# Own PSUM banks for the shift row, Wo's first product copied into the second's banks, and a new hand-kept order of all engines

## The chip, the cores and the metric

The kernel runs on one core of a Trainium2 chip. The metric is the device time of one execution in microseconds, median over runs. All times below are microseconds (us) unless marked otherwise. Engines are named as in the profile: PE (TensorE, matmuls), DVE (VectorE), ACT (ScalarE), POOL (GpSimd, which here mostly issues DMAs and does small steps), SP (SyncE, which issues DMAs).

## What is computed

One transformer block with adaptive LayerNorm: S = 2048 rows, D = 1024 columns, 32 heads, F = 3584.

```python
mod = silu(c) @ w_mod                      # six vectors: sa, ca, ga, sb, cb, gb
h = layernorm(x) * (1 + ca) + sa
q, k, v = split_heads(h @ wqkv)            # 32 heads of 32
pq, pk = phi(q), phi(k)                    # phi(t) = (t + 1 if t > 0 else exp(t)) + 1e-6
kv = sum over s of pk[s] (x) v[s];  z = sum over s of pk[s]
o = (pq @ kv) / (pq @ z + 1e-6)
x = x + ga * (o @ wo)
h = layernorm(x) * (1 + cb) + sb
x = x + gb * ((gelu(h @ w_gate) * (h @ w_up)) @ w_down)
```

Inputs and outputs are bfloat16.

## The kernel before

**Phases.** The code runs `kvq_phase` (first LayerNorm, K, V, K/V products per head, Q), `merge_phase` (numerators and denominators of the attention), `wo_phase` (output projection, residual, second LayerNorm), and then for each of two groups of 1024 rows `gate_up(g)` and `down_out(g)`. The 2048 rows are four blocks b = 0 to 3 of 512 rows; a group is two blocks. Most large products are not done as eight half-size block products but as seven (`seven`, with stages `s1` to `s7`), with sums and differences of blocks made beforehand by DVE. In the feed-forward part some of the seven are split in seven once more. So PE has fewer matmuls, and DVE has many additions (line 788, the helper `tt_op`, which records every addition of two tensors).

**PSUM.** It has eight banks of 512 fp32 columns. `Banks(lo, hi)` is a ring over some of them: each call hands out the next. Two rings that share a bank make their users wait for each other. `psK0 = Banks(4, 7)` is the ring of the K products of block 0 (`k_group`: eight matmuls at line 1248, then ACT takes Exp at 1254 and Relu at 1255, and DVE adds them). `psR` is the ring of `shift_row`; before, it is bank 7 alone.

**Shift row.** V of the first block is multiplied without the additive part `sa` of the modulation. `shift_row` makes up for it: DVE spreads `sa` (line 1034), sixteen matmuls (`row_sums`, line 860) multiply it with Wv, ACT copies the row, and two adds (`add(0)`, `add(1)`: one matmul at line 1042 and four DVE steps each) put it on the K/V sums. All three take their bank from `psR`.

**Modulated columns.** `hr1[0]` is the first block's normalized input, transposed; at the end of `start_phase` its eight column tiles are scaled and shifted, by DVE (line 1028) or for every third tile by ACT. The K groups of block 0 read them. Beside them, `ln1_block(1)` makes statistics of the next block (lines 866 and 868).

**Wo.** Blocks 0 and 1 go through `wo_tile`, eight plain tiles (matmuls at line 1526), each followed by ACT and DVE statistics and a normalized copy. Those copies go to DRAM scratch `xhs` and come back transposed (`h2_load`, line 1462, one load for each half of the group), and are then modulated in `h2_mod` (ACT at line 1504, DVE at 1506) into the operand of gate and up. Blocks 2 and 3 go through `wo_stages`, a seven-product (matmuls at line 1590). `QA`, `QB`, `QC`, `QD` are the bank pairs 0-1, 2-3, 4-5, 6-7. In `s1` the first product P1 is made in pair A, and ACT copies it (`fcopy`, line 1093, 1024 fp32 columns) to SBUF; A is then kept and accumulated on. In `s2` the second product is made in pair B, and `comb` adds P1 from SBUF to it (DVE, PSUM and SBUF) and that sum to the residual (DVE, SBUF only). In `s3` A is accumulated on and copied once more (`fcopy`). `s5` copies each half at line 1125.

**Gate, up, down.** `gate_up` uses lines 1705 (plain products) and 1716 (the products split once more), with seeds from one PSUM bank to another by ACT (line 1761) and Gelu at 1780; `down_out` uses lines 1921 and 1966 and ends with the output.

**Order.** The code doesn't issue as it runs. `Plan` records each instruction with what it reads and writes; `Plan.order` plans all five engines with a cost for each kind of instruction, and `Plan.refine` then moves instructions by hand-kept tables, `SHIFTS`: for each engine a list that says for each place by how many places the instruction that stands there was moved ("z13" stands for thirteen zeros). The instructions are issued in that order on each engine, with semaphore waits where one depends on another. So on each engine the order is fixed, and an instruction that waits holds back all behind it on its engine. Two instructions on the same engine also wait for each other by semaphore where the second reads what the first wrote.

Of the kernel before, what the change touches and what calls it, by code (L numbers as in the profile page):

```python
# [508 lines left out]
def kernel(  # L509
# [581 lines left out]
    def fcopy(ring, ps):  # L1091
        t = ring()
        ac.activation(out=t, in_=ps, func=AF.Copy)  # L1093
        return t

    def seven(mm, comb, direct, A, B, slots=(0, 1, 2), ring=None):


        st = {}
# [8 lines left out]
        def s1():  # L1108
            st["pa"] = products(A.pair(), "a11", "b11", True)
            st["p1"] = fcopy(p1_at, st["pa"])  # L1110
# [1082 lines left out]
```

## Time and profile before

| | us |
|---|---|
| runs | 737.71, 737.94, 739.62 |
| median | 737.94 |
| the profiled execution | 738.96 |
| its span on the core | 737.2 |
| mean granted PE clock in it | 0.997 |

The profiled execution is the one that all rows are from; its span is from the first instruction to the last, the rest of its time lies around that. The timeline's rows give start and duration in us from the span's start, the engine, the line, the operation, output and input, shapes and count, and in brackets the idle time before it and what ended it. Neighbouring rows of the same kind are drawn together (x36). A matmul row's end is modelled, so the next row can start before it. "L788" is the line of the helper for additions, whoever calls it.

### The profile page before, as it was taken

How to read it: one execution, taken by the hardware profiler on the slowest of the kernel's cores; microseconds unless marked ns; L12 is line 12 of the kernel's file. 1: busy time of each engine (PE TensorE's matmuls, PEld its weight loads, DVE VectorE, ACT ScalarE, POOL GpSimd, SP SyncE). 2: the span in 40 equal slices, each digit the busy share in tenths (PEclk: the TensorE clock that was granted, in tenths of full speed). 3: DMA queues.
4: the chain of work that ended last, by engine and by line, in shares of the span. 5: the costliest groups of instructions: out<-in, count | busy, mean ns of one | idle time of the engine just before them, and what ended most of it. 6: DMA issues, size and time to landing. Idle time of an engine off the chain costs nothing.

```text
span 737.2 us, 12148 instructions
## 1 busy us (share of the span) xinstructions
PE 724.6 (98%) x4365; PEld 404.5 (55%) x4365; DVE 658.0 (89%) x1472; ACT 457.3 (62%) x829; POOL 103.2 (14%) x174
## 2 busy tenths in 40 slices
PE   8999999999999999999999999999999999999997
PEld 4444545444444555555555667545555555568674
DVE  5699998797799999999997799987897899999998
ACT  5566666679787799999776712026677776742110
POOL 2325631120121012311300000000000010000000
PEclk9999999999999999999999999999999999999999
DMA  9976855999999477768867788645242455599992
GB/s 313 329 200 161 240 102 126 312 275 280 303 249 315 174 226 239 190 203 255 240 176 246 208 278 270 219 168 175 91 140 103 140 175 175 169 258 284 269 278 86
DMA packets 160988, 159.26 MB, mean 216 GB/s; under 512 B 34208, under 2 KB 140448, under 8 KB 160288
## 3 DMA queue, kind: packets, MB, share of 16 engines
q1 hardware_dynamic: 143568, 122.30, 55.4%
q0 software_dynamic: 14848, 33.82, 15.3%
q10 hardware_dynamic: 2512, 2.36, 1.0%
q8 instruction: 34, 0.56, 0.3%
q14 instruction: 26, 0.21, 0.1%
HBM read 122.42 MB, written 36.04 MB: 215 GB/s over the span
## 4 chain that ended last, share of the span: by engine, by line
PE 78%; DVE 13%; issue 3%; DMA 2%; ACT 2%; POOL 1%; DVEq 0%; SPq 0%; ACTq 0%; POOLq 0%
PE psum L1705 28%; PE psum L1716 10%; PE psum L1921 8%; DVE mem L788 8%; PE psum L1966 8%; PE psum L1149 8%; PE psum L1219 7%; PE psum L1526 3%; PE psum L1590 2%; PE psum L923 2%; DVE mem L866 1%; DMA mem<-xhs 1%; PE psum L1263 1%; DMA xhs<-mem 1%; PE psum L1248 1%
## 5 line engine op out<-in xcount | busy, mean ns | idle before, releaser
L788 DVE TENSOR_TENSOR mem<-mem 128x256 f16<-128x256 f16 (+14 forms) x857 | 380.8, 486 | 19.9 <-ACT mem L1093 4.5
L1705 PE MATMUL psum<-mem 128*128 128x512 f16 x1144 | 273.9, 379 | 0.0
L1093 ACT ACTIVATE mem<-psum 128x512 f32<-128x512 f32 (+3 forms) x320 | 167.4, 557 | 131.6 <-PE psum L1966 36.8
L788 DVE TENSOR_TENSOR mem<-psum,mem 128x512 f16<-128x512 f32 (+5 forms) x213 | 159.8, 757 | 23.5 <-PE psum L1149 7.3
L1705 PEld LDWEIGHTS <-mem 128*128 128x128 f16 (+1 forms) x1144 | 111.7, 98 | 102.8 <-issue 1.4
L1716 PE MATMUL psum<-mem 128*128 128x256 f16 x742 | 106.9, 272 | 0.9 <-DVE mem L788 0.6
L1716 PEld LDWEIGHTS <-mem 128*128 128x128 f16 (+1 forms) x742 | 72.3, 98 | 43.9 <-issue 2.6
L1966 PE MATMUL psum<-mem 128*128 128x256 f16 (+1 forms) x784 | 88.7, 273 | 0.2 <-ACT mem L1093 0.2
L1966 PEld LDWEIGHTS <-mem 128*128 128x128 f16 x784 | 76.6, 98 | 12.8 <-DVE mem L788 0.4
L1921 PE MATMUL psum<-mem 128*128 128x512 f16 (+2 forms) x350 | 75.2, 370 | 1.0 <-DVE mem L788 1.0
L1149 PE MATMUL psum<-mem 128*128 128x512 f16 (+1 forms) x280 | 63.2, 379 | 0.0
L788 DVE TENSOR_TENSOR psum<-psum,mem 128x256 f32<-128x256 f32 x106 | 44.8, 429 | 15.9 <-ACT mem L1093 9.5
L1761 ACT ACTIVATE psum<-psum 128x512 f32<-128x512 f32 x56 | 32.6, 584 | 38.3 <-DVE mem L788 26.5
L1921 PEld LDWEIGHTS <-mem 128*128 128x128 f16 x350 | 34.2, 98 | 37.0 <-issue 1.2
L1219 PE MATMUL psum<-mem 128*128 128x512 f16 x224 | 51.6, 379 | 0.0
L1149 PEld LDWEIGHTS <-mem 128*128 128x128 f16 x280 | 27.1, 98 | 32.1 <-DVE mem L1052 0.4
L1780 ACT ACTIVATE mem<-psum 128x512 f16<-128x512 f32 x56 | 33.1, 597 | 10.3 <-PE psum L1705 10.0
L1219 PEld LDWEIGHTS <-mem 128*128 128x128 f16 (+1 forms) x224 | 21.5, 98 | 25.7 <-issue 0.8
L1790 ACT ACTIVATE mem<-mem 128x512 f16<-128x512 f16 x56 | 34.9, 631 | 0.8 <-DVE mem L788 0.8
L1327 POOL DMA_DIRECT2D ts<-in_B_w_down_dram x28 | 29.0, 1335 | 6.9 <-DMA ts<-in_B_w_down_dram 6.5
L1248 PE MATMUL psum<-mem 128*128 128x512 bf16 x128 | 29.6, 379 | 0.2
L1526 PE MATMUL psum<-mem 128*128 128x512 f16 x128 | 28.2, 379 | 0.0
(143 smaller groups left out, 577.4 us busy)
## 6 DMA issues: line engine op xcount, KB each, us to landing
mem<-in_B_w_gate_dram SPq DMA_DIRECT2D x14, 1024.0 KB, 7.8
mem<-in_B_w_up_dram SPq DMA_DIRECT2D x14, 1024.0 KB, 6.0
mem<-in_w_mod_dram SPq DMA_DIRECT2D x24, 512.0 KB, 8.5
mem<-us SPq DMA_DIRECT2D x24, 448.0 KB, 8.7
mem<-ts SPq DMA_DIRECT2D x5, 1792.0 KB, 9.4
ts<-in_B_w_down_dram POOLq DMA_DIRECT2D x28, 256.0 KB, 6.5
mem<-in_B_w_down_dram SPq DMA_DIRECT2D x15, 448.0 KB, 6.4
mem<-in_A_x_dram SPq DMA_DIRECT2D x23, 256.0 KB, 5.7
```

Source lines behind the costliest of these rows:

```text
L788: ve.tensor_tensor(out=out, in0=a, in1=b, op=op)
L1093: ac.activation(out=t, in_=ps, func=AF.Copy)
L1149: te.matmul(ps, lhsT=A[:, k, i * P:(i + 1) * P], rhs=B[:, k, :], start=(start and k == 0), stop=(k == KH - 1), skip_group_check=True)
L1219: te.matmul(o, lhsT=W[:, k, (j0 + i) * P:(j0 + i + 1) * P], rhs=h_form(a, k), start=(start and k == 0), stop=(k == KH - 1), skip_group_che ...
L1248: te.matmul(ps, lhsT=hr1[b][:, k, tl * P:(tl + 1) * P], rhs=Wk[:, k, n * NW:(n + 1) * NW], start=(k == 0), stop=(k == KD - 1))
L1526: te.matmul(psw[:, half, :], lhsT=pqT[b][:, g, tl * P:(tl + 1) * P], rhs=Wp[:, g, half * NW:(half + 1) * NW], start=(g == 0), stop=(g == K ...
L1705: te.matmul(ps, lhsT=a[:, k, e, :], rhs=b[:, k, :], start=(start and k == 0), stop=(k == KH - 1), skip_group_check=True)
L1716: te.matmul(ps, lhsT=self.x[a][:, k, :], rhs=self.y[y][:, k, :], start=(start and k == 0), stop=(k == KH // 2 - 1), skip_group_check=True)
L1780: ac.activation(out=o, in_=ps, func=AF.Gelu_apprx_tanh)
L1790: ac.activation(out=o, in_=o, func=AF.Gelu_apprx_tanh)
L1921: te.matmul(psm[:, q, c], lhsT=A[:, i, q * P:(q + 1) * P], rhs=wt[:, i, c], start=(start and i == 0), stop=(i == NPR - 1), skip_group_chec ...
L1966: te.matmul(ps[:, q, :], lhsT=a[:, k, q * P:(q + 1) * P], rhs=y[:, k, :], start=(start and q == 0 and k == 0), stop=(k == NPR // 2 - 1), s ...
```

## The change

Three things, in the diff in this order after the tables:

1. `psR` becomes `Banks(2, 3)`: the row sums and the two adds of `shift_row` use banks 2 and 3 and no longer bank 7.
2. `seven` gets an argument `first`. With it (Wo alone), ACT copies P1 from pair A into pair B, PSUM to PSUM, and the second product's matmuls accumulate on that (their `start` is off). One DVE addition (`direct(0)`) then adds the sum to the residual, where `comb` had two. For block 2 the two pairs change places (QD, QC).
3. All five lists of `SHIFTS` are new, so that the order on every engine is a new one. They were made with an instruction's wait on an earlier instruction of its own engine counted. The planner's own costs are not changed.

PE, ACT, POOL and SP have as many recorded instructions as before; DVE has two fewer (1457 for 1459 recorded). On PE 736 stretches of matmuls stand at another place, most of them by a few groups of four or eight matmuls. The largest moves that are spoken of below: the sixteen row sums go behind four K groups; both adds of the shift row stand late, where the second stood; on ACT the copies of P1 and of `s3` and `s5` of block 2 and P1 of block 3 go ahead of all of `h2_mod`; eight matmuls of the last Wo tile go between `s1` and `s2` of block 2.

```diff
 SHIFTS = {
     "PE": (
-        "z13 8 8 -2 -2 -2 -2 4 4 4 4 4 4 4 4 4 4 4 4 4 4 4 4 4 4 4 4 4 4 4 4 4 4 4 4 4 4 4 4 -34 -34 -34 -34 4 4 4 4 "
...
     "DVE": (
-        "z1 2 -1 -1 z1 1 3 -2 3 -2 2 -1 1 1 1 1 2 z1 1 1 5 -13 -1 -1 -1 -1 z4 1 -1 z2 1 -1 1 -1 5 7 1 1 6 1 12 5 5 2 "
...
+        "z1 2 2 -2 2 6 -4 -2 -1 z1 2 3 -2 -5 -1 z1 1 3 z2 -4 4 -1 -1 -1 -1 z9 2 -1 -1 5 7 1 4 6 -1 3 4 -2 3 3 3 3 3 "
...
@@ -751,7 +752,7 @@
-    psD, psS, psR = Banks(5, 5), Banks(7, 7), Banks(7, 7)
+    psD, psS, psR = Banks(5, 5), Banks(7, 7), Banks(2, 3)
@@ -1093,7 +1094,7 @@
-    def seven(mm, comb, direct, A, B, slots=(0, 1, 2), ring=None):
+    def seven(mm, comb, direct, A, B, slots=(0, 1, 2), ring=None, first=None):
@@ -1107,10 +1108,17 @@
         def s1():
             st["pa"] = products(A.pair(), "a11", "b11", True)
-            st["p1"] = fcopy(p1_at, st["pa"])
+            if first is None:
+                st["p1"] = fcopy(p1_at, st["pa"])
+            else:
+                st["pb"] = B.pair()
+                ac.activation(out=st["pb"], in_=st["pa"], func=AF.Copy)
 
         def s2():
-            comb(products(B.pair(), "a12", "b21", True), st["p1"], 0, 0)
+            if first is None:
+                comb(products(B.pair(), "a12", "b21", True), st["p1"], 0, 0)
+            else:
+                first(products(st["pb"], "a12", "b21", False))
@@ -1603,11 +1611,14 @@
-        def direct(ps):
-            tt_op(dst(1, 0), ps, dst(1, 0), ALU.add)
-            store(1)
-
-        return seven(mm, comb, direct, *((QC, QD) if b == 2 else (QA, QB)), ring=wf_ring)
+        def direct(row):
+            def out(ps):
+                tt_op(dst(row, 0), ps, dst(row, 0), ALU.add)
+                if row:
+                    store(1)
+            return out
+
+        return seven(mm, comb, direct(1), *((QD, QC) if b == 2 else (QA, QB)), ring=wf_ring, first=direct(0))
```

357 rows, old and new, of the table SHIFTS are left out of this document.

## The prediction

> **What bounds the kernel now.** I read the page first: the busy times and the chain that ended last.
>
> ```profile
> PE 724.6 (98%) x4365; PEld 404.5 (55%) x4365; DVE 658.0 (89%) x1472; ACT 457.3 (62%) x829; POOL 103.2 (14%) x174
> ...
> PE 78%; DVE 13%; issue 3%; DMA 2%; ACT 2%; POOL 1%; DVEq 0%; SPq 0%; ACTq 0%; POOLq 0%
> ```
>
> TensorE is busy for 724.6 of a 737.2 us span and carries 78% of the chain. VectorE is next with 658.0 us. The change leaves all 4365 matmuls in place, so what it can gain is PE's idle time alone, 12.6 us at most, and part of that is the start and the end. So the second view is PE's list of waits, the eight longest of twelve (columns: us in total, times, longest).
>
> ```profile
> PE psum L902 <- POOL mem masks.py:199: 1.5, 1, 1.5
> PE psum L1042 <- ACT mem L1255: 1.2, 1, 1.2
> PE psum L1590 <- ACT mem L1093: 1.2, 1, 1.2
> PE psum L1921 <- DVE mem L788: 1.0, 1, 1.0
> PE psum L909 <- DVE mem L895: 0.9, 1, 0.9
> PE psum L1263 <- DVE mem L788: 0.7, 1, 0.7
> PE psum L909 <- ACT mem L911: 0.7, 1, 0.7
> PE psum L1716 <- DVE mem L788: 0.6, 1, 0.6
> ```
>
> These eight single waits add up to 7.8 us. L902 and the two of L909 (3.1 us) are the start, before any product that the change touches. The other five are 4.7 us: L1042 (shift row), L1263 (K/V products), L1590 (Wo), L1716 (gate and up) and L1921 (the last down products). The third view is the engines' busy time in stretches of 40 us, for how near VectorE comes to PE there (columns: core, window, PE, PEld, DVE, ACT, POOL, granted clock, DMA).
>
> ```profile
> 200.00:240.00 40.00, 38.80 (x180) 17.47 (x179) 37.66 (x58) 30.55 (x57) 8.01 (x14) 1.00 1.05 285
> 240.00:280.00 40.00, 40.00 (x224) 21.65 (x223) 39.58 (x96) 33.20 (x66) 2.72 (x5) 1.00 0.55 184
> 280.00:320.00 40.00, 39.38 (x228) 22.14 (x227) 38.83 (x108) 37.74 (x77) 13.26 (x14) 1.00 0.79 242
> 320.00:360.00 40.00, 39.67 (x230) 22.26 (x229) 38.25 (x104) 35.87 (x74) 7.52 (x14) 1.00 0.70 217
> ```
>
> From 240 to 360 us VectorE is busy for 39.58 + 38.83 + 38.25 = 116.66 of 120 us: it has 3.34 us to spare, and PE loses 0.62 + 0.33 = 0.95 us. There a gain for PE alone is worth little unless VectorE's own line gets shorter.
>
> **Part 1, shift row (banks and place).** The timeline's PE rows, then the VectorE rows, of the first block's K groups (start, duration, and in brackets the wait before):
>
> ```profile
> 29.51 1.05 PE L860 MATMUL psum<-mem 128*32 128x512 bf16 x16 [0.19 <-DMA mem<-in_A_x_dram]
> 30.50 12.86 PE L1248 MATMUL psum<-mem 128*128 128x512 bf16 x56
> 44.57 0.38 PE L1042 MATMUL psum<-mem 128*128 128x512 f16 x1 [1.21 <-ACT mem L1255]
> ```
> ```profile
> 29.38 1.05 DVE L1028 TENSOR_SCALAR mem<-mem 128x512 f16<-128x512 f16 x3
> 30.34 0.69 DVE L866 BATCH_NORM_STATS2 mem<-mem 128x6 f32<-128x512 bf16 x1
> ...
> 31.26 0.21 DVE L868 BATCH_NORM_AGGREGATE mem<-mem 128x2 f32<-128x12 f32 x1
> ```
>
> L1042 waits 1.21 us for a relu of a K group (L1255), because it takes bank 7 from K's ring of banks 4 to 7. With banks 2 and 3 its own, that releaser is gone. In the new order both adds stand where the second stood (about 72 us), far from the K groups. Gain 1.2 us, and up to 0.2 more of small gaps.
>
> Against this: the sixteen row sums (L860, 1.0 us at 29.51) now come after four K groups, so PE wants the first modulated columns (L1028) at 29.5 instead of 30.5. On VectorE a BATCH_NORM_STATS2 (0.60 from start to start, 30.34 to the next) and two aggregates (0.2 each) now stand ahead of these columns; the first is ready at about 29.4 + 0.6 + 0.4 + 0.35 = 30.7. PE then waits 1.2 us where it did useful row sums. Behind the columns on VectorE everything slides by about 1 us, and the copy that feeds the row sums is due at 37.4, just when PE gets there. Sum: -1.4 + 1.2 = -0.2. Bounds: -1.4 if the columns are in time, +1.0 if the row sums also have to wait. I take -0.2, from the rows.
>
> **Part 2, Wo's first product.** Five fences follow: the timeline's PE rows and ACT rows around the wait, the piece of the chain that ended last, VectorE's rows, and the page's group of copies from PSUM to PSUM (56 of them, 32.6 us busy, 584 ns each):
>
> ```profile
> 228.09 7.97 PE L1590 MATMUL psum<-mem 128*128 128x512 f16 x36 [1.20 <-ACT mem L1093]
> ...
> 243.26 3.62 PE L1705 MATMUL psum<-mem 128*128 128x512 f16 x16
> ```
> ```profile
> 221.34 1.01 ACT L1093 ACTIVATE mem<-psum 128x1024 f32<-128x1024 f32 x1
> 224.70 1.52 ACT L1504 ACTIVATE mem<-mem 128x512 f16<-128x512 f16 x2 [2.35 <-DMA mem<-xhs]
> 226.13 1.91 ACT L1093 ACTIVATE mem<-psum 128x1024 f32<-128x1024 f32 x2
> ...
> 229.21 0.60 ACT L1125 ACTIVATE mem<-psum 128x512 f32<-128x512 f32 x1 [0.47 <-PE psum L1590]
> ```
> ```profile
> 217.10 7.58 DMA mem<-xhs
> ```
> ```profile
> 224.43 2.48 DVE L788 TENSOR_TENSOR mem<-mem 128x1024 bf16<-128x1024 bf16 x4
> ...
> 236.11 0.41 DVE L1506 TENSOR_SCALAR mem<-mem 128x512 f16<-128x512 f16 x1
> 236.43 1.22 DVE L788 TENSOR_TENSOR mem<-psum,mem 128x1024 bf16<-128x1024 f32 x1
> ```
> ```profile
> L1761 ACT ACTIVATE psum<-psum 128x512 f32<-128x512 f32 x56 | 32.6, 584 | 38.3 <-DVE mem L788 26.5
> ```
>
> This is one chain: the transposed load takes 7.58 us, ACT idles 2.35 us for it, does two modulations of the next stage (L1504), and only then the two copies (226.13) that free PE at 228.09. The new ACT order has both first-product copies and the second copy (s3) before any modulation. So the chain's DMA link leaves PE's path: -1.2. Could the copy into PSUM bring its own wait? Half the width costs 0.584 us there (L1761), so the whole is between 1.01 (the old copy's row) and 1.17; I take 1.01, the same width. The second product now needs it, but eight Wo tile matmuls (8 x 7.97/36 = 1.8 us) stand between in block 2, and another stage of eight in block 3, which cover 1.17. If that cover failed, the full copy would show, twice. Value -1.2, bounds 0 and -1.4. VectorE loses, for each of the two blocks, one 1024-wide pass of 2.48/4 = 0.62 us; the read from PSUM (1.22) stays. That is 1.2 us off an engine that is near its limit from 240 us on.
>
> Its cost: the last Wo tile comes 1.8 us later, and its statistics stand behind a copy of 1.01, so its half of the transposed load comes up to 2.8 us later. That is the slower rival.
>
> **Part 3, the order elsewhere.** K/V products (L1263, 0.7): half of it, -0.3, as its releaser is the same VectorE queue, with h's columns moved within it. Gate and up of the first group: PE's 0.95 us there end at VectorE, which is freed of 1.2 us just before and has fewer instructions right behind the one they depend on. I take -0.5, bounds 0 and -0.95. What such neighbours cost shows near the end:
>
> ```profile
> 714.18 0.69 DVE L788 TENSOR_TENSOR mem<-psum,mem 128x512 f16<-128x512 f32 x1
> 714.79 4.01 DVE L788 TENSOR_TENSOR mem<-mem 128x512 f16<-128x512 f32 x7
> 718.72 0.68 DVE L788 TENSOR_TENSOR mem<-psum,mem 128x512 f32<-128x512 f32 x1
> 719.44 2.94 DVE L788 TENSOR_TENSOR mem<-mem 128x512 f16<-128x512 f32 x5
> ```
>
> From 714.18 the next starts 0.61 us later, before the 0.69 is over; its input is not the one just written. From 718.72 the next, which adds to that result, starts 0.72 us later. So a neighbour's wait on its own engine costs 0.11 us. Counted in the two orders, VectorE has 148 such pairs before and 137 after; in the last 100 us 25 and 19. Six fewer are 0.7 us of VectorE in the tail, where it sets PE's 1.0 us wait of L1921. I take -0.5, bounds 0 and -1.7. Over the whole kernel eleven fewer are only 1.2 us.
>
> The Trainium skill, page "VectorE: DVE Perf Modes", section "The DRAIN you can't avoid", says otherwise: eight copies with a semaphore after each took as long as eight with one at the end, so the semaphore costs nothing extra. By it the re-ordering would bring nothing in the tail and the sum would be 0.5 us less, 735.9. The rows of this trace disagree by 0.11 us a pair, on two-input adds, and I go by them.
>
> Last, some 700 runs of matmuls change places, most by one to three groups, each able to meet an operand that is not yet there. Where a result goes from PE through ACT or VectorE and back, the distance in PE's order is no shorter than before, so I take +0.2; bounds 0 and +3, the latter being three waits like the longest ones here.
>
> **Sum.** -0.2 - 1.2 - 0.3 - 0.5 - 0.5 + 0.2 = -2.5 us against the profiled execution's 738.96, which is 1.0 above the median 737.94 of the runs; carried to the median it is 735.4.
>
> **Rivals.**
> - *All of it goes.* Every wait that the change touches: -1.4 - 1.4 - 0.7 - 0.95 - 1.7 = -6.15, so 731.8. For it: each is a single wait with a named releaser. Against: the late first columns in part 1, and VectorE's 3.34 us of slack.
> - *The gain is given back.* Only the wait of Wo goes, and VectorE, full from 240 to 360 us, hands PE the same time later, as the 1.2 us that PE arrives earlier exceeds the 0.42 us VectorE is idle in 240 to 280. What stays is some 0.4 to 0.8: about 737.4. It also covers the case that the re-ordering does not do what it says, as eleven pairs in 148 are few.
> - *Slower: the second half of the transposed load blocks ACT.* In the new ACT order three modulations of that half stand ahead of the copy that opens the gate products, and that copy's reader is the row at 243.26. ACT comes to them at 229.21 - 1.2, plus eight modulations of 0.72 (1.43 us for the two at 224.70), one copy of 0.95 (1.91 for the two at 226.13) and five of 0.58: 237.6. It needs 2.7 us from there, and PE comes to the reader at 242.06, so the load may land at 239.3. Before, it was there at 236.11 at the latest (first use); 2.8 later is 238.9, just in time. Each us beyond 239.3 stops PE, and behind these modulations wait the copy, then all of ACT's gelus. At the price of the first half's transfer again (7.58) it lands at 246.5 and PE stops 7.2 us: -2.5 + 7.2 = +4.7, 742.6. It decides for slower from 244.0 on. For it: the DMA share of 1.05 in 200 to 240. Against: 236.11 is an upper bound of the landing.
>
> **How the numbers follow.** Around 0.3%, 2.2 us, is what the runs can tell from no change; so faster means under 735.7, slower above 740.2. The forecast case has 0.45, and lies on the line: 0.30 of it faster, 0.15 the same. All of it goes: 0.20, faster. Given back: 0.21, the same. Slower: 0.14, with the new waits of part 3 at their upper bound (+3) and the load. That is 0.50 faster, 0.36 the same, 0.14 slower. The predicted time is that of the likeliest case, 735.4. The range reaches down to 731.8, the first rival, and up to 739.8, where the sum meets its bad bounds in part 1 (+1.2), Wo (+1.2) and the moved runs (+2.8) all but 0.8; it leaves out most of the slower case and a little below.
>
> **What would show it.** Right: PE's waits without L1042 and L1590, a wait of about 1 us at L1248 near 30 us in their place, ACT's first modulation after the copies at about 229, PE's first gate product 1.2 to 1.5 us earlier than 240.67, VectorE two instructions fewer. Wrong: PE waiting on ACT between 238 and 246, a new wait over 1 us anywhere after 250, or a head whose K groups start later than 31.

## The result and the profile after

| | before | changed |
|---|---|---|
| median, us | 738.97 (6 runs, 737.71 to 739.62) | 734.01 (6 runs, 733.09 to 736.13) |
| ratio | | 0.9942, 95% interval 0.9925 to 0.9959 |
| the profiled execution, its span | 738.96, 737.2 | 735.55, 733.5 |

The change makes the kernel faster by 0.58% (0.41 to 0.75%): 4.3 us by the means, of which the ratio is made, 5.0 by the medians. 735.4 was forecast, 2.5 us under the 737.94 of the three earlier runs: the way is right, the size about half of what came. The tables and the code are of other lengths, so the lines move a little: L789 is the helper of additions (788 before), L1256 the K groups (1248), L1598 Wo's seven-product (1590), L1932 the last down products (1921). In the kernels of the experiments they move by up to ten more.

The page's busy times and the chain that ended last, after:

```profile
PE 723.0 (99%) x4352; PEld 405.7 (55%) x4365; DVE 652.4 (89%) x1470; ACT 455.6 (62%) x829; POOL 101.5 (14%) x174
...
PE 91%; ACT 3%; DMA 2%; DVE 2%; issue 1%; POOL 1%; SPq 0%; DVEq 0%; ACTq 0%
```

VectorE's share of the chain falls from 13% to 2%, TensorE's rises from 78% to 91%. PE shows 4352 matmuls for 4365, because 13 records are missing from the trace; its weight loads are complete, and progress is told by them below. DVE has the two instructions fewer. PE's list of waits, after (us in total, times, longest):

```profile
PE psum L903 <- POOL mem masks.py:199: 1.5, 1, 1.5
PE psum L933 <- DMA mem<-in_w_mod_dram: 1.4, 2, 0.9
PE psum L817 <- DVE mem L812: 0.8, 1, 0.8
PE psum L1256 <- DVE mem L1029: 0.8, 1, 0.8
PE psum L910 <- ACT mem L912: 0.7, 1, 0.7
PE psum L1932 <- DVE mem L789: 0.5, 1, 0.5
PE psum L1256 <- ACT mem L927: 0.2, 1, 0.2
PE psum L1256 <- DVE mem L1053: 0.2, 1, 0.2
```

The shift row's wait, Wo's, that of the K/V products and both of gate and up are gone. L1932 keeps half of its 1.0 us. New are 1.2 us at the K groups (L1256, three rows; the one for L1053 stands at 48.38, 16 us behind the two for the columns), 0.8 at L817 (a modulation row between the first Wo tiles, at 198.39; the DVE copy that it needs stands behind an addition for which DVE waits 4.9 us until a load of x lands), and 1.4 at L933, the scale columns of the start, which now wait for a weight load.

Where the time went shows best when the k-th weight load of PE is compared in the two traces. The differences to the profile before, in us, taken at places where both kernels have issued the same products (negative is earlier); "again" is a second profile of the changed kernel, the others are experiments told below:

| stretch (time before) | after | again | no_copy | start_old | warm_more |
|---|---|---|---|---|---|
| start, to 16 us | +2.2 | +0.8 | +0.9 | -1.5 | -0.9 |
| K groups, shift row, K/V: to 75 | -1.5 | -1.5 | -1.5 | -0.9 | -1.5 |
| to the last Wo tiles, 202 | +0.5 | +0.5 | +0.4 | +0.4 | -0.2 |
| Wo, to 253 | -1.5 | -1.3 | -0.8 | -1.5 | -0.4 |
| first gate and up, to 390 | -1.3 | -1.5 | -0.7 | -0.7 | -1.5 |
| first down, second gate and up, to 629 | -0.9 | +0.2 | -0.9 | -0.9 | -0.9 |
| last down, to 732 | -1.1 | -1.1 | -1.1 | -1.1 | -1.1 |
| sum | -3.7 | -4.1 | -3.8 | -6.3 | -6.5 |

Behind the start the changed kernel wins 5.9 us in the first profile and 4.8 in the second. The start gives back 2.2 and 0.8 of it. That loss was in no term of the prediction.

**The start.** Stretches of 2 us, before and then after; the third column from the end is the granted clock:

```profile
10.00:12.00 2.00, 1.32 (x11) 0.96 (x10) 1.62 (x8) 1.81 (x4) 0.00 (x0) 0.50 1.10 353
12.00:14.00 2.00, 2.00 (x8) 0.80 (x7) 1.99 (x7) 1.97 (x6) 0.00 (x0) 0.69 1.10 348
14.00:16.00 2.00, 2.00 (x17) 1.17 (x16) 0.88 (x2) 0.70 (x3) 0.00 (x0) 1.00 1.11 355
```
```profile
8.00:10.00 2.00, 0.72 (x23) 0.64 (x23) 1.22 (x5) 0.14 (x1) 0.00 (x0) 1.00 1.08 373
10.00:12.00 2.00, 1.31 (x25) 1.15 (x22) 0.75 (x4) 0.98 (x3) 0.00 (x0) 0.53 1.10 353
12.00:14.00 2.00, 2.00 (x10) 0.93 (x8) 1.93 (x7) 1.97 (x3) 0.00 (x0) 0.50 1.10 349
14.00:16.00 2.00, 2.00 (x8) 0.83 (x7) 0.64 (x3) 1.29 (x5) 0.00 (x0) 0.50 1.10 352
16.00:18.00 2.00, 2.00 (x11) 0.96 (x10) 0.88 (x2) 0.00 (x0) 0.00 (x0) 0.77 1.06 383
```

Both kernels run PE at half clock for a while, after a stretch in which PE is often idle (0.72 us busy of 2 from 8 to 10 us, after). In slices of 0.4 us the low stretch is from 9.8 to 13.2 us before, 3.4 us long, and from 10.1 to 16.9 after, 6.8 us long. Products run at half speed there, so by half of its length (an estimate) it costs 1.7 us before and 3.4 after. PE's rows of the timeline after show it (start, duration):

```profile
11.53 1.01 PE L910 MATMUL psum<-mem 128*128 128x128 f16 x8 [0.69 <-ACT mem L912]
12.34 3.62 PE L924 MATMUL psum<-mem 128*128 128x512 f16 x8
```

Eight products take 3.62 us, where the same shape takes 1.89 later on. The Trainium skill, page "TensorE: Matmul & The Clock Gate", section "Part 1: The HAM clock gate (the "warmup" mystery)", says that the clock is halved after an idle window of about 3.4 us and raised after a busy one, and that these windows run freely. The stretches agree: 3.4 us before, 6.8 after, 3.4 in the second profile of the same kernel, so one window or two. That PE need not be idle for a whole window is what the trace adds: in the 3.4 us ahead of the low clock PE was busy for 2.2 us before and for 1.9 after. The idle share alone does not decide it either: with the old order of the start (start_old below) PE was busy for 1.6 us from 7.0 to 10.4 us, and the clock stayed at 1.00.

The profiled execution, 735.55, lies 1.5 us over the median of its runs, about what one such window costs. The other executions show only their mean clock, and it goes with the time: of the twelve of the changed kernel, here and in the run that repeats it, four at 0.995 (two windows in 733 us give that) took 735.2 us in the mean, seven at 0.997 or 0.998 took 733.9, and one at 1.00 took 732.1. The kernel before was at 0.995 in three of the eleven executions beside the repeated run, so a second window is not peculiar to the new order.

**Wo.** PE and ACT after (PE's row is one piece of 88 products with no wait; before, it was cut at 228.09), SP's row of the second half's transposed load, and, from the view of that load alone, the time from its start to its landing:

```profile
219.22 19.16 PE L1598 MATMUL psum<-mem 128*128 128x512 f16 x88
```
```profile
223.74 1.01 ACT L1115 ACTIVATE psum<-psum 128x1024 f32<-128x1024 f32 x1
225.47 1.02 ACT L1094 ACTIVATE mem<-psum 128x1024 f32<-128x1024 f32 x1 [0.72 <-PE psum L1598]
...
230.28 4.33 ACT L1512 ACTIVATE mem<-mem 128x512 f16<-128x512 f16 x6
...
239.38 2.21 ACT L1512 ACTIVATE mem<-mem 128x512 f16<-128x512 f16 x3
```
```profile
232.75 3.79 SPq L1470 DMA_TRANSPOSE mem<-xhs  x1
```
```profile
DMA to landing us min/median/max: 5.8/5.8/5.8
```

The copies stand ahead of the modulations (L1512), whose first start at 230.28 without a wait for the load. The copy from PSUM to PSUM takes 1.01 us, as assumed. SP's row ends at 236.5, but the load lands at 232.75 + 5.8 = 238.6; three modulations of the second half start at 239.38, 0.8 us later. In the second profile of the changed kernel it lands at 236.2 and they start at 238.17.

**Gate and up.** The stretches that the prediction showed, after:

```profile
240.00:280.00 40.00, 40.00 (x226) 21.89 (x225) 39.37 (x96) 34.19 (x69) 3.71 (x5) 1.00 0.73 233
280.00:320.00 40.00, 40.00 (x235) 22.70 (x233) 38.95 (x110) 38.10 (x78) 12.04 (x16) 1.00 0.85 260
320.00:360.00 40.00, 40.00 (x234) 22.57 (x232) 37.88 (x106) 35.17 (x74) 8.77 (x12) 1.00 0.57 184
```

PE is busy throughout, and DVE, with 116.2 us of 120, is as full as before.

### The profile page after: what moved, and what is told of

Same layout as the page of the kernel before. It is cut to its first block, busy times and chain, and to the rows that moved or that the text cites. A ratio compares the mean times of both kernels' runs of the same rounds, so it can differ in the third digit from the quotient of the medians.

```text
span 733.5 us, 12117 instructions
## 1 busy us (share of the span) xinstructions
PE 723.0 (99%) x4352; PEld 405.7 (55%) x4365; DVE 652.4 (89%) x1470; ACT 455.6 (62%) x829; POOL 101.5 (14%) x174
## 4 chain that ended last, share of the span: by engine, by line
PE 91%; ACT 3%; DMA 2%; DVE 2%; issue 1%; POOL 1%; SPq 0%; DVEq 0%; ACTq 0%
PE psum L1716 33%; PE psum L1977 12%; PE psum L1727 11%; PE psum L1932 10%; PE psum L1157 8%; PE psum L1227 5%; PE psum L1598 3%; PE psum L1534 3%; PE psum L1256 2%; PE psum L924 2%; DVE mem L789 1%; DMA mem<-in_A_x_dram 1%; DMA mem<-in_w_mod_dram 1%; PE psum L1271 1%; ACT mem L1317 0%
## 5 line engine op out<-in xcount | busy, mean ns | idle before, releaser
L789 DVE TENSOR_TENSOR mem<-mem 128x256 f16<-128x256 f16 (+12 forms) x855 | 377.9, 484 | 17.9 <-ACT mem L1094 4.6
L1094 ACT ACTIVATE mem<-psum 128x512 f32<-128x512 f32 (+3 forms) x318 | 165.0, 552 | 138.3 <-DVE mem L789 38.2
L789 DVE TENSOR_TENSOR mem<-psum,mem 128x512 f16<-128x512 f32 (+5 forms) x213 | 159.3, 756 | 34.3 <-ACT mem L1094 5.6
L1727 PE MATMUL psum<-mem 128*128 128x256 f16 x742 | 107.4, 272 | 0.0
L1727 PEld LDWEIGHTS <-mem 128*128 128x128 f16 (+1 forms) x742 | 72.4, 98 | 43.1 <-issue 0.8
L1932 PE MATMUL psum<-mem 128*128 128x512 f16 (+2 forms) x348 | 75.2, 370 | 0.6 <-DVE mem L789 0.5
L1932 PEld LDWEIGHTS <-mem 128*128 128x128 f16 x350 | 34.2, 98 | 36.0 <-issue 0.7
L789 DVE TENSOR_TENSOR psum<-psum,mem 128x256 f32<-128x256 f32 x106 | 44.6, 427 | 8.7 <-ACT mem L1094 8.3
L1256 PE MATMUL psum<-mem 128*128 128x512 bf16 x123 | 29.0, 380 | 1.4 <-DVE mem L1029 0.8
```

The lines of the kernel that those rows point to most:

```text
L789: ve.tensor_tensor(out=out, in0=a, in1=b, op=op)
L1256: te.matmul(ps, lhsT=hr1[b][:, k, tl * P:(tl + 1) * P], rhs=Wk[:, k, n * NW:(n + 1) * NW], start=(k == 0), stop=(k == KD - 1))
L1727: te.matmul(ps, lhsT=self.x[a][:, k, :], rhs=self.y[y][:, k, :], start=(start and k == 0), stop=(k == KH // 2 - 1), skip_group_check=True)
L1932: te.matmul(psm[:, q, c], lhsT=A[:, i, q * P:(q + 1) * P], rhs=wt[:, i, c], start=(start and i == 0), stop=(i == NPR - 1), skip_group_chec ...
```

## The experiments

Each is timed beside the kernel before on the same chip. Where only the order is changed, the lists of the code are new, and the edit is shown as the sequence of lines.

**The same kernel again.** No edit.

> The changed kernel unchanged, with a profile of its own. In the first profile PE was 2.2 us behind the kernel before at 20 us, with the granted clock at 0.50 from 10 to 16 us (before: to 13 us). If the new order of the start is the cause, this profile shows PE 2 us behind again and a low clock until about 16 us. If it is chance of the run (where the DMAs land, where the clock's switch falls), it shows 0 to 1 us, and the time of that execution is 1 to 2 us under 735.55. Median expected 734.0 in both.

Measured: 734.52, ratio 0.9929 (0.9912 to 0.9947). PE is 0.8 us behind at 16 us, not 2.2; the clock is low from 11.4 to 14.8 us. The low stretch is as long here as in the profile before (3.4 us), so these 0.8 us are not the clock's but the new order's own; the 1.4 us more in the first profile go with its second window. So the loss in the start differs between executions of one kernel. The time of this profiled execution, 735.03, is only 0.5 us under 735.55, not 1 to 2: a wait of 0.9 us in the second gate and up (L1727), which the first profile does not have, takes most of it back.

**The old order of the start.** PE's lines (count) in the start:

```diff
 975 903x6 910x4 933x32 910x12
-924x8 910x4 924x8 910x8 933x32 910x4 924x36
+924x8 910x4 924x4 910x4 924x4 910x8 933x32 924x36
```

> The changed kernel, but the instructions of the start (statistics of the first rows, their transposes, the scale columns, V of the first block) stand in the order of the kernel before, on every engine; all else as changed. If the new order of the start costs 2 us, the median falls by 1 to 2 us under the changed kernel (732 to 733) and PE reaches the K groups at about 30.5 instead of 32.3. If the loss is chance, the median is within 0.5 us of it (733.5 to 734.5).

Measured: 732.98, ratio 0.9919 (0.9901 to 0.9936), beside 734.52 of the same kernel with its new start on this chip; the two intervals overlap. In the profile the clock is 1.00 throughout and PE is 1.5 us ahead at 16 us. 0.7 of that is lost again in the K groups: PE comes to them earlier and waits 1.8 us for the first column, 0.8 in the changed kernel. One of the five executions, 735.13 at a mean clock of 0.995, shows that the old start can meet the low clock too. So the new start has no gain to show, and likely costs.

**Wo without the copy into PSUM.** The shift row's banks and all orders as changed, block 2's bank pairs again as before; the two DVE additions of each block stand where the one stood:

```diff
-        return seven(mm, comb, direct(1), *((QD, QC) if b == 2 else (QA, QB)), ring=wf_ring, first=direct(0))
+        return seven(mm, comb, direct, *((QC, QD) if b == 2 else (QA, QB)), ring=wf_ring)
```

> The changed kernel's banks and order, but Wo's first product goes to SBUF as before and the second product is added by two DVE instructions. Theory that the copy into PSUM brings Wo's gain: PE's wait at Wo comes back, 1.2 us, or DVE's 1.2 us more show up in the gate and up products: median 735.0 to 735.6. Theory that the order alone brings it (the copies stand ahead of the modulations): 734.0 to 734.4, no wait of PE at Wo over 0.4 us.

Measured: 735.00, ratio 0.9946 (0.9931 to 0.9960); the changed kernel beside it 734.52. PE's row at Wo:

```profile
226.87 10.69 PE L1596 MATMUL psum<-mem 128*128 128x512 f16 x48 [0.27 <-DVE mem L794]
```

A wait of 0.27 us, for DVE, is what is left of the 1.20. In the table Wo wins 0.8 without the copy and 1.3 to 1.5 with it. So the order, the copies ahead of the modulations, brings more than half, and the copy into PSUM some 0.5 us. By the medians alone the copy is not told from nothing. In the first gate and up this kernel wins 0.7 for 1.3 and 1.5, with a wait of 0.7 us at L1722; start_old, which has the copy, has one of 0.8 there, so this is not put down to the copy.

**The banks alone.** The kernel before with one line, and the adds moved to where the new banks allow them:

```diff
-    psD, psS, psR = Banks(5, 5), Banks(7, 7), Banks(7, 7)
+    psD, psS, psR = Banks(5, 5), Banks(7, 7), Banks(2, 3)
```

> The kernel before with one part of the change: the shift row has banks 2 and 3. Its two adds (two matmuls, eight DVE steps) had to move: they stand right ahead of what uses these banks next; all else in the old order. Theory that the shared bank is the cause of the shift row's wait: L1042's 1.2 us go, median 1.0 to 1.3 us under the kernel before. Theory that the gain up to 75 us comes from the order: 0 to 0.3 us under it, a wait of like size elsewhere between 40 and 75 us.

Measured: 748.38, ratio 1.0114 (1.0088 to 1.0141): slower by 9 us, which neither theory had. PE's waits:

```profile
PE psum L1156 <- DVE mem L1052: 3.7, 2, 2.5
PE psum L867 <- ACT mem L933: 3.1, 1, 3.1
```

L1042's wait of 1.2 us is gone, but the row sums (L867 here) wait 3.1 us until ACT has emptied bank 2, which V of the first block used just before, and V's products (L1156) wait 3.7 us for DVE to read the adds out of the banks that they share now. Around the longest of these waits the clock falls too: it is at 0.50 on the mean from 76 to 78 us and at 0.75 from 78 to 80. So the banks are worth something only with row sums and adds moved behind, as the new order has them: the two parts of the change can't be taken apart.

**More products that compute nothing, in the new start and in the old.** In the new start eleven (2, 2, 4, 3), in the old one eight (4, 1, 0, 3):

```diff
         keep_warm(4)
+        keep_warm(2)
         start_tile(0, xh[0])
         keep_warm(2)
+        keep_warm(2)
         scale_cols(0, 0, KH, psc[0])
+        keep_warm(4)
         scale_cols(0, KH, KD, psc[0])
+        keep_warm(3)
         start_tile(1, xh[1])
```

> The changed kernel with eleven more matmuls that compute nothing (of the kind at L903, 0.2 us each at full clock) in the places of the start where PE waited: two ahead of the first transposes, two and four ahead of the two groups of the scale columns (L933), three ahead of the second transposes. Theory that the clock is lowered because PE is idle for 2 to 3 us between 7 and 11.5 us: the granted clock stays 1.00 from 10 to 20 us, the 8 matmuls of L924 that took 3.6 us take 1.9, median 732.0 to 732.8. Theory that the start is bound by the landing of the weights and its clock is a symptom: PE reaches the K groups as late as before, median 734 to 735.

> The kernel with the old order of the start (start_old) and eight more such matmuls: four ahead of the first transposes, one ahead of the scale columns, three ahead of the second transposes. Clock theory: the executions of about 735 that start_old had now and then are gone, all within 731.5 to 733. The other theory: as start_old, 732 to 735.

Measured: 732.86 (ratio 0.9915, 0.9889 to 0.9941) and 731.99 (0.9906, 0.9880 to 0.9932). In the profile of the first the clock stays up:

```profile
10.00:12.00 2.00, 1.96 (x18) 1.03 (x16) 1.39 (x6) 1.63 (x4) 0.00 (x0) 1.00 1.09 360
12.00:14.00 2.00, 2.00 (x14) 1.05 (x13) 1.83 (x7) 1.97 (x5) 0.00 (x0) 1.00 1.10 348
```

PE is 0.9 us ahead at 16 us instead of 0.8 to 2.2 behind: the landing of the weights does not set the start, and most of the loss goes with the low clock. Not all of it: start_old, at full clock too, is 1.5 us ahead, so 0.6 us stay with the new order. The time falls by less than the start wins, by the ratios 1.0 to 2.0 us. This kernel comes to Wo earlier, while the transposed load comes when it comes; ACT and then PE wait for it:

```profile
228.65 4.34 ACT L1521 ACTIVATE mem<-mem 128x512 f16<-128x512 f16 x6 [1.97 <-DMA mem<-xhs]
```
```profile
233.94 1.89 PE L1607 MATMUL psum<-mem 128*128 128x512 f16 x8 [0.99 <-ACT mem L1103]
```

The copy of block 3's third stage (L1103) stands behind six modulations, so the wait that Wo lost is back with 0.99 us at another product. For warm_old an execution of 734.30 remained, against its expectation. It is the profiled one, its clock is up, and two other waits stand in its list (L822 is L817 of the changed kernel, L1736 is in gate and up):

```profile
PE psum L822 <- DVE mem L817: 1.3, 1, 1.3
PE psum L1736 <- DVE psum L794: 1.2, 1, 1.2
```

So not every late execution is the clock's.

**More DVE neighbours that depend on each other, and moves alone.** 27 moves by one to three places in the first gate and up stage; in the first kernel each puts an addition right behind the one that it reads, in the second none does (in outline):

```diff
 addition a
-another addition
 addition b, which reads what a wrote
+another addition
```

> The changed kernel with 27 DVE instructions of the first gate and up stage moved by one to three places, so that 27 more DVE instructions stand right behind the one whose result they read (18 before, 45 then, in that stage). By the rows (0.11 us a pair) DVE needs 3.0 us more where it has about 3.8 us to spare in 240 to 360: gate and up end 0.5 to 2.5 us later than in the changed kernel and than in the run with moves alone. By the rule that such a wait costs nothing: within 0.5 us of the run with moves alone.

> The control for pairs_more: as many DVE instructions of the same stage are moved by as many places (2 by one, 11 by two, 14 by three), with no more and no fewer such pairs. Both theories: 0 to 1 us over the changed kernel, for what comes later than it did; the difference to pairs_more is what the pairs cost.

Measured: 741.93 (12 runs, ratio 1.0036, 1.0014 to 1.0058) and 739.87 (12 runs, 1.0014, 0.9996 to 1.0032). Both lose the whole gain, and the control alone costs 5 to 6 us by the ratios, far over the 0 to 1 expected. PE's waits in gate and up, with the additional pairs and then with moves alone:

```profile
PE psum L1721 <- DVE mem L794: 3.9, 5, 1.2
```
```profile
PE psum L1721 <- DVE mem L794: 1.3, 3, 0.5
PE psum L1732 <- DVE psum L794: 1.2, 2, 0.9
```

The pairs cost 2.1 us between the medians, but the intervals overlap, and in the two profiles the kernels end within 0.4 us of each other. So by the total time the price of a pair stays open. The rows of the trace are firmer: of two additions in a row, an independent one starts 0.083 us before the first one's end (median of 1041, after), a dependent one 0.035 us behind it (median of 115; from 0.034 to 0.035 between the tenth and the ninetieth percentile). With 27 more, 142 pairs show the same 0.035. A pair costs DVE 0.12 us. The Trainium skill's section "The DRAIN you can't avoid" (page "VectorE: DVE Perf Modes") has a semaphore after each of eight copies cost nothing extra; on these additions the wait for a direct neighbour does cost, and the measurement decides. The rows after tell what it is not. 26 additions that read nothing of the one in front, but overwrite what it read or wrote, start 0.035 us behind its end just the same, so it is not the read. And 109 that wait on DVE's own semaphore for an instruction further back start 0.083 us before the end of the one in front, so it is not a semaphore as such: the price is paid where an addition must wait for the end of its direct neighbour.

**The first gate and up in the old order.** The instructions of that stage in their old order among themselves, all else as changed; 22 had to go further forward where the two orders meet.

> The changed kernel, but the instructions recorded in the first gate and up stage stand in the order of the kernel before among themselves, on every engine (22 of them had to go a few places further forward, where the two orders meet). PE won 1.3 us in this stage. Theory that the stage's own order wins it, by 11 fewer DVE pairs (11 x 0.12 = 1.3 us of DVE): median 1.0 to 2.0 us over the changed kernel (735.2 to 736.5). Theory that it comes from the 1.2 us of DVE that Wo saves just before: 0 to 0.4 us over it.

Measured: 766.88, ratio 1.0387 (1.0360 to 1.0414). From 253 to 390 us PE loses another 1.8 us to the kernel before, but most is lost at the two ends of the stage, in a few long waits for DVE (below) and in the low clock around them (a mean of 0.51 from 246 to 253 us, 0.53 from 423 to 434, 0.51 from 444 to 451):

```profile
PE psum L1982 <- DVE mem L794: 12.6, 1, 12.6
PE psum L1721 <- DVE mem L794: 9.6, 3, 5.4
```

An old order in new surroundings measures the seam. Which part of the new order wins the 1.3 us in this stage is not settled by it.

**The columns first.** One move on DVE:

```diff
-854 867 869 1029 869 1029 1029 1029 1029 1029
+854 1029 1029 1029 1029 1029 1029 867 869 869
```

> The changed kernel with one DVE move: the six modulated columns of the first block (L1029) stand right behind the shift they need, ahead of a statistics instruction and two aggregates of the next block. If the columns' place is what PE waits for there (0.8 us at L1256, 0.2 behind it), K starts 0.7 us earlier and the median falls by 0.5 to 0.8. If the statistics then come late for the next block, a wait of the same size appears between 40 and 75 us and the median stays.

Measured: 735.67, ratio 0.9958 (0.9942 to 0.9974), no gain. PE's rows:

```profile
29.52 0.39 PE L1261 MATMUL psum<-mem 128*128 128x512 bf16 x1 [0.16 <-DVE mem L1034]
30.37 6.65 PE L1261 MATMUL psum<-mem 128*128 128x512 bf16 x30 [0.45 <-ACT mem L1031]
36.95 1.05 PE L866 MATMUL psum<-mem 128*32 128x512 bf16 x16
39.35 6.85 PE L1261 MATMUL psum<-mem 128*128 128x512 bf16 x30 [1.36 <-ACT mem L1267]
```

The wait for the first column falls from 0.81 to 0.16 us, and a wait of 1.36 us for the Exp of a K group on ACT (L1267) stands some 9 us behind it. The waits moved, and their sum did not fall: 0.16 + 0.45 + 1.36 = 1.97 us for 0.81 + 0.23 = 1.04.

**Columns first in the kernel warm_old ("best"), and warm_old once more.** In best the same DVE move is made in the old start, with the columns in the order in which K reads them:

> Old order of the start with the eight idle-filling matmuls, and the six columns first and in the order in which K reads them. Expected: the 1.8 us wait at the first K group shrinks to 0.5, PE 1.2 us ahead of the run warm_old2 from there on, median 730.5 to 731.3. Rival: the next block's statistics, 1.9 us later, take it back by 75 us, median as warm_old2.

> The kernel of warm_old once more, on the same chip as best, to compare the two: 731.5 to 732.5 if the old start with a clock that stays up is worth 2 us against the changed kernel, 734 if the earlier 732.0 was that chip's.

Measured: 733.49 (ratio 0.9926, 0.9910 to 0.9943) and 733.16 (0.9929, 0.9909 to 0.9949). The columns bring nothing here either: the wait of 1.8 us for the first column, which warm_old2 has, is gone, and waits at the K groups of 1.2 us for a weight load and of 1.1 for ACT stand in its place. And warm_old, 0.9906 on one chip, is 0.9929 on another. The kernels with a changed start have the lowest ratios, 0.9906 to 0.9929, against 0.9929 and 0.9942 for the changed kernel; the intervals overlap, so a version that beats it is likely, by 1 to 2 us, but not shown.

## Why the prediction was right, and where it was not

- *The bound.* Right in the main: the time is PE's waits. DVE's share of the chain fell with them, as it would if it had carried those waits. What it left out is the clock: at 0.50 PE is busy and loses time all the same, an estimated 1.7 us before, and no list of waits shows that.
- *Shift row and K/V (-0.2 and -0.3).* The mechanism is right, the size too small: -1.5 in both profiles of the changed kernel. The new wait for the columns was put at 1.2 and is 0.81 + 0.23 = 1.04, so that is nearly right (of the two aggregates only one stands ahead of the first column); the first part of it, less the 0.19 that PE waited there before, is the 0.6 us by which PE falls further behind at 29.5 us, now that no row sums stand there. What was missed is on the other side: L1263's 0.7 went wholly, not by half, and the row sums do not wait at all at 39.46.
- *Wo (-1.2).* Right: -1.3 to -1.5, and the load that held PE is off its path; PE's first gate product starts at 239.51, 1.2 us earlier than the 240.67 before. The text gave no split between copy and order; the profiles put more than half on the order.
- *Gate and up (-0.5, bounds 0 and -0.95).* Mis-sized: -1.3 and -1.5, past the bound. The bound was the busy time that was missing in two stretches of 40 us; ends of matmuls are modelled, so short gaps between their starts need not show in it, which is a likely reason but not a shown one. Which part of the new order wins here stays open. The second gate and up and the first down win up to 0.9 more, which no term had.
- *The tail (-0.5).* Right in kind, -1.1 in size; L1932's wait fell by 0.5. But the reason was wrong: from 640 us on the two orders have 29 and 28 dependent pairs, not six fewer. The pairs are fewer in the first gate and up (25 and 16 from 240 to 390 us). What wins the other 0.6 in the tail no run takes apart.
- *The price of a pair (0.11).* It holds, 0.12, in 115 to 142 pairs. It was put against the Trainium skill's rule, and the rows were the better guide for the duration; how much of it reaches the end time is open.
- *New waits (+0.2, up to +3).* They came: 0.8 at L817, and a single 0.7 to 0.9 in gate and up in some of the profiles.
- *The start.* The missing step. It was left out as "before any product that the change touches", but the order of the start is new as well: 0.6 to 0.9 us of delay are its own, and one more window of the low clock made it 2.2 us in the profiled execution. So one of the text's own signs of being wrong came about, a head whose K groups start later than 31: they start at 32.27 there, at 30.85 in the second profile.
- *The rivals.* The gain was not given back. The slower case did not come, but it was near: the load of the second half landed at 238.6, where 238.9 was reckoned as the latest, and ACT came to it at 239.38. That the two agree is partly luck. The load was issued 7.0 us later than before (232.75 for 225.7), not 2.8 at the most; it was the first use at 236.11, an upper bound of the old landing, that had hidden the slack. The mechanism is real all the same: the load of the first half held ACT and PE again, by 0.99 us, once the start was sped up.

Sum of the terms against what they were: -2.5 forecast; -5.9 and -4.8 behind the start, +2.2 and +0.8 in it. So it is in part luck that the forecast time lies within 1.4 us of the median: the terms behind the start were too small together, and the start, which had no term, gave some of it back.

## What to carry to other kernels

When an order is made anew, the start belongs to the sum too: short waits that lie close together there can cost a whole stretch at half clock, and that shows in the granted clock of stretches of 2 us, not in the list of waits. Where a shared bank makes a wait, look at who used the new bank just before: here the bank without the new order cost 9 us, and only bank and order together won. A DMA's row on the queue that issues it is not its landing: in the trace after, 3.79 us against 5.8. A wait that is taken from a queue can be handed on within 10 us (the columns) or come back when the work ahead of it gets faster (the transposed load), so ask of each what is late next.

## What the runs showed of the hardware that was not expected

- The low clock of the start comes in stretches of 3.4 or 6.8 us, with PE idle for only a part of the time before; with eleven products that compute nothing, 0.2 us each, the start is at 1.00 in the profile, and all six executions are at 0.999 or 1.00 in the mean.
- An addition on DVE that must wait for its direct neighbour's end starts 0.035 us behind it, whether it reads the result or only overwrites; one that waits on DVE's own semaphore for an older instruction starts 0.083 us before the neighbour's end, as one without a wait does.
- An order so tight is easily lost: 27 of DVE's 1457 instructions, moved by at most three places, took 5 to 6 us.
- A copy of 128x1024 fp32 from PSUM to PSUM by ACT takes 1.01 us, the same as to SBUF.
